# Pooled values in small tiles of their own, the gate written in place, and feature buffers moved by 32 bytes

## The chip, the cores and the metric

One NeuronCore of a Trainium2 chip runs the whole program. The metric is the device time of one execution in microseconds (us); a kernel's time is the median of several runs. Five engines work side by side, each with its own stream of instructions: TensorE (PE in the profile; its weight loads are PEld), VectorE (DVE), ScalarE (ACT), GpSimd (POOL) and SyncE (SP), which here only issues DMA transfers. They meet through semaphores.

## The reference

Attention with pooled keys and values over 8 batches of 8 heads (576 positions, 64 features each) is followed by two feed-forward layers over 4608 tokens of 512 features, everything in 32-bit floats.

```python
k_p = k.reshape(B, H, Sp, pool, D).mean(axis=3)      # pool = 8, Sp = 72
v_p = v.reshape(B, H, Sp, pool, D).mean(axis=3)
scores = scale * np.matmul(q, k_p.transpose(0, 1, 3, 2))
attn = softmax(scores)                               # over the 72 pooled positions
x = heads_to_features(np.matmul(attn, v_p))          # 4608 x 512

h = x @ w_in                                         # 512 -> 2048
x = (h * np.clip(h + 3.0, 0.0, 6.0) / 6.0) @ w_out   # 2048 -> 512

g = x @ w_gate                                       # 512 -> 1536
val = x @ w_val
return (g / (1.0 + np.exp(-g)) * val) @ w_out        # 1536 -> 512
```

## The kernel before

**Arithmetic.** Matmuls run in a reduced 32-bit type. Each operand is therefore cut into a high part (a rounding copy) and a low part (what is left), and a product takes three matmuls: high with high, high with low, low with high. `split` (L147, L148) makes the two parts: ACT copies the high one, VectorE subtracts for the low one. Three of the four large products also use a seven-product block scheme (Strassen's, with the names P1 to P7 for the products, 11 to 22 and S1 to S4 for the sums of features, 11 to 22 and T1 to T4 for those of weights).

**Stages.** (1) Start-up, to about 125 us: attention of the first 512 tokens. (2) To about 603 us: nine blocks of 512 tokens. For each block 16 iterations of the `up` product (`mm3` at L616, 12 matmuls of 512 columns), and between them the attention of the next block. ACT writes the clipped part of an iteration's result to a tile `t` (L627, in `act1`), VectorE multiplies it by the result into `g` (L632, in `gate1`), and SP stores `g` to device memory (L636, `store_g`). In the loop `gate1` of an iteration runs in the next one, and its `store_g` in the one after that. (3) To about 969 us, the down stage: `down_b` (L885), 9 blocks of tokens x 7 products, each product 48 matmuls of 256 columns. (4) To the end: the second layer, with an up product of 384 columns (`mm3x` at L706) and a down product of 256 columns on the same line.

**One pair of heads ("a head" below: 32 of them, 4 for each batch) in stages 1 and 2.** SP loads the keys (`load_k`, L313), the values (`load_v` and `fetch_v`, L326 and L327, two DMAs into a tile of 128 pooled positions x 8 x 64) and the tail of the values (`load_vtail`, L333, three DMAs of the 16 pooled positions that don't fit in 128, each copy 32 partitions further on). The work of a head is cut into steps: RK and K pool and transpose the keys; R0 (`prep_v`) pools the values on POOL by three adds, 8 to 4 to 2 to 1 (L440 in `pool_v`), and writes the pooled row times a mask (L447) into slots 4 and 5 of the same value tile; R1 pools the tail with the same `pool_v`; R (`split_v`, L453 and L454) writes the high parts on ACT; Q (`split_v_lo`, L460 and L462) the low parts on VectorE and, as its last act, plans the loads of the values and the tail of the head three places on (`next_v`). Value tiles have three buffers, tails have three (`vts_t`).

**One unit of queries.** S scores (matmuls, L496 is one form), X and A exponentials, M (`scale_e`, L544, POOL) the division by the sum, E and F the tail of the exponentials (`split_tail`, and `lo_tail` at L559, on POOL and VectorE in turn), T the transposes on TensorE (`transpose_a`; L570 transposes the tail), U and L the copies to high and low parts, V the product with the values (`attend`, from L594), W and Y the writes of the high (L605) and low (L609) part of `x`. P (`prep_q`, L478) prepares queries, whose loads (`fetch_q`, L381) it plans two segments ahead.

**What sets the order.** The order of instructions on every engine is written out by the program (`manual_schedule`). A table `when` gives every step of a unit a place in time; sorting these gives one list of steps, `steps`, about twenty to a unit. `before(...)` asserts that a step comes ahead of another. Loads are not issued at once: a step puts them on a list `later` with a due count, `done[0] + 4` or `+ 8`, and they are emitted on SP's queue that many steps further on. SP works through its queue in order, so an instruction that waits holds up all behind it: on that one queue are the loads of q, k and v, the stores of `g`, and the loads and stores of the weight preparation (`prep_slot`: loads by `fetch_into`, L121; splits at L273 and L276; stores to `sup` and `sw` at L280 and L285).

**Weights and features of the down stage.** The features come back by `load_g` (L844) into tiles `gq`, and `split` makes from them the tiles `gb`, four buffers of 4 KB a partition, four `gb` tiles to a product. The seven weight blocks `pw` lie in big buffers that are free by then: one in a tile of its own, `px`, on the right side of memory, the others in the buffers of the up stage's weights (`wu`, four) and of `x` (two). The matmul takes its weights from `pw` and its moving operand from `gb`. `evac_b` (L901 and after it) takes the results.

**Start addresses.** From the memory plan of the built program, in bytes within a partition, and their remainder modulo 64: `wu` starts at 17088 + 16384 k (0), `x` at 82624 and 99008 (0), `gb` at 115392 + 4096 k (0), `px` at 178144 (32), `gq` at a remainder of 32. In the second layer the ring that holds `wr` and `xc` starts at 32, and `gc` at 0. The pools on the left side follow one another upwards (`wu`, `x`, `gb`, then `t` and its like), those on the right side downwards, so `px` lies above `gq`.

Of the kernel before, what the change touches and what calls it, by code (L numbers as in the profile page):

```python
# [8 lines left out]
F32 = mybir.dt.float32  # L9
# [14 lines left out]
def kernel(  # L24
# [47 lines left out]
    x_p = left_b.enter_context(tc.tile_pool(name="x", bufs=2))  # L72
    gb_p = left_b.enter_context(tc.tile_pool(name="gb", bufs=4))
# [10 lines left out]
    half = const.tile([P, 1], F32, name="half")  # L84

# [217 lines left out]
    vts_t = [a_p.tile([96, POOL, D], F32, name=f"vts{i}") for i in range(3)]  # L303
# [25 lines left out]
    def load_vtail(b, p, eng):  # L329
        v1 = v[b, 2 * p + 1].rearrange("(s o) d -> s o d", o=POOL)  # L330
        vts = vts_t[(b * KT + p) % 3]
        for i in range(3):
            eng.dma_start(out=vts[32 * i:32 * i + TAIL], in_=v1[P - SP_:])  # L333
        vt_t[b, p] = vts
# [102 lines left out]
    def pool_v(t):  # L437
        n = POOL // 2
        while n:
            nc.gpsimd.tensor_tensor(out=t[:, 0:n], in0=t[:, 0:n], in1=t[:, n:2 * n], op=ALU.add)  # L440
            n //= 2

    def prep_v(b, p):
        t = v_t.pop((b, p))
        pool_v(t)
        m = t[:, 4:6]
# [178 lines left out]
    def act1(ps):  # L625
        t = t_p.tile([P, N], F32, tag="t", name="t")
        nc.scalar.activation(out=t, in_=ps, func=ACTF.Relu, bias=half, scale=1.0 / 6.0)  # L627
        return t

    def gate1(t, ps):  # L630
        g = t_p.tile([P, N], F32, tag="g32", name="g32", bufs=4)
        nc.vector.scalar_tensor_tensor(out=g, in0=t, scalar=1.0, in1=ps, op0=ALU.min, op1=ALU.mult)  # L632
        return g
# [388 lines left out]
    for i, h in ((i, head_no[u[0], p]) for i, u in enumerate(units) for p in u[1]):  # L1022
# [8 lines left out]
        if h + 3 < len(heads) and h >= KT - 1:  # L1031
            before(("Q", h), ("R1", h + 3))
    for i, u in enumerate(units):
# [34 lines left out]
    def next_v(i):  # L1068
        for load in (load_vtail, load_v):
            for h in next_heads(i, 3):  # L1070
                later.append((done[0] + 4, lambda load=load, h=h: load(*heads[h], nc.sync)))

    def do_step(st):
# [9 lines left out]
        elif what == "R0":  # L1083
            prep_v(*heads[i])
        elif what == "R1":
            pool_v(vt_t[heads[i]])
        elif what == "R":
            split_v(*heads[i])
        elif what == "Q":
            split_v_lo(*heads[i])  # L1090
            next_v(i)
        elif what == "P":
            prep_q(segs[i])
            for n in ((KT, KT + 1) if i == KT - 1 else (i + 2,)):
                if KT <= n < len(segs) and i >= KT - 1:
                    later.append((done[0] + 4, lambda n=n: load_q(segs[n], sync4)))
# [40 lines left out]
    with tc.manual_schedule():  # L1137
# [64 lines left out]
        for j in range(NB):  # L1202
            for f in range(F1):
                if (j, f) == (NB - 1, 0):
# [4 lines left out]
                    new_pw(0, lb["px"].tile([P, BIG], F32R, tag="px", name="pw"))  # L1209
# [125 lines left out]
```

## Time and profile before

| | |
|---|---|
| runs | 1761.25, 1763.97, 1765.88 us (median 1763.97) |
| the profiled execution | 1764.89 us |
| its span in the profile | 1763.1 us |
| mean granted clock of TensorE | 0.988 |
| busy share of the span | PE 97%, PEld 91%, DVE 76%, ACT 43%, POOL 36% |
| matmuls | 11116 |
| bytes moved | 432.47 MB, 245 GB/s on average |

Times in the profile are microseconds from the start of the span. Matmuls are pipelined, so the busy time that a row gives for one matmul (some 280 ns) is longer than the pitch at which they follow each other; where TensorE runs without a gap, the busy time of a group divided by its count is the pitch. The granted clock is a share of full speed (1.00 is 2.4 GHz). In rows of waits and groups, "<-DVE gb L142" names the engine, tile and line that ended the wait. An issue of a DMA on SP is written SPq.

### The profile page before, as it was taken

Reading aid. Unit: us, or ns where it says so; the run is one execution under the profiler, and the core shown is the slowest. Engines: PE = TensorE matmul, PEld = TensorE weight load, DVE = VectorE, ACT = ScalarE, POOL = GpSimd, SP = SyncE. Lnnn points to the kernel's source line nnn. Section 1 sums busy time; section 2 is a strip of 40 time slices with the busy share of each in tenths; the row PEclk is TensorE's granted clock in tenths of the full one; section 3 lists DMA queues with packets and bytes.
Section 4 is the critical chain, followed back from the end, with each engine's and each line's share of the span. In section 5 each row is a group of like instructions: output and inputs, shape, how many; then the busy total and the mean of one; then the engine's idle time right before and its main releaser. Section 6 shows DMA issues by size and latency. Waiting matters only on the chain.

```text
span 1763.1 us, 30766 instructions
## 1 busy us (share of the span) xinstructions
PE 1705.5 (97%) x11116; PEld 1608.8 (91%) x11116; DVE 1333.7 (76%) x2356; ACT 753.8 (43%) x1656; POOL 638.4 (36%) x822
## 2 busy tenths in 40 slices
PE   5889998999999999999999999999999999999999
PEld 3678887878788899999999999999999999999999
DVE  6797887888875678888888668668668668668666
ACT  5565554545544445555554224224224224224223
POOL 6565666666722000000000550550550550550560
PEclk9799999999999999999999999999999999999999
DMA  6776888878767974555565778878878878878876
GB/s 162 183 188 171 245 257 259 243 256 247 223 223 255 413 308 150 187 208 196 194 213 200 263 249 269 313 244 272 314 240 281 307 243 278 310 244 276 275 239 215
DMA packets 235832, 432.47 MB, mean 245 GB/s; under 512 B 86688, under 2 KB 168608, under 8 KB 218528
## 3 DMA queue, kind: packets, MB, share of 16 engines
q1 hardware_dynamic: 234624, 430.25, 73.9%
q8 instruction: 88, 1.44, 0.3%
q14 instruction: 64, 0.52, 0.1%
q10 hardware_dynamic: 1056, 0.26, 0.1%
HBM read 326.11 MB, written 104.33 MB: 244 GB/s over the span
## 4 chain that ended last, share of the span: by engine, by line
PE 76%; DMA 3%; DVE 3%; issue 1%; ACT 1%; SPq 0%; POOL 0%; DVEq 0%; ACTq 0%; POOLq 0%
PE b L706 45%; PE b L885 19%; PE h L616 10%; DMA g<-g 2%; PE pss L496 1%; DMA gq<-g 1%; DVE g L632 1%; PE pst L570 0%; DVE s L276 0%; PE pst L566 0%; DMA q_in<-in_q_dram 0%; SPq L381 0%; DVE q L139 0%; DVE xc L148 0%; PE psv L594 0%
## 5 line engine op out<-in xcount | busy, mean ns | idle before, releaser
L706 PE MATMUL b<-xc,wr 128*128 128x384 f32 x3024 | 526.3, 334 | 3.5 <-ACT xc L147 2.3
L706 PEld LDWEIGHTS b<-xc,wr 128*128 128x128 f32 x3024 | 523.9, 188 | 4.7 <-ACT xc L147 3.1
L616 PE MATMUL h<-x,wu 128*128 128x512 f32 x1728 | 435.3, 403 | 4.7 <-DVE g L632 2.6
L753 POOL TENSOR_TENSOR s<-s,c 128x384 f32<-128x384 f32 x144 | 142.4, 1014 | 756.6 <-ACT s L751 756.6
L715 DVE TENSOR_TENSOR c<-c,b 128x384 f32<-128x384 f32 x504 | 264.9, 552 | 174.7 <-PE b L706 151.0
L616 PEld LDWEIGHTS h<-x,wu 128*128 128x128 f32 x1728 | 322.7, 192 | 72.3 <-DVE g L632 4.9
L885 PEld LDWEIGHTS b<-gb,pw 128*128 128x128 f32 x3024 | 362.2, 191 | 0.5 <-DVE gb L148 0.4
L885 PE MATMUL b<-gb,pw 128*128 128x256 f32 x3024 | 362.5, 283 | 0.2 <-DVE gb L148 0.2
L706 PE MATMUL b<-wr,gc 128*128 128x256 f32 x2268 | 265.6, 279 | 0.0
L706 PEld LDWEIGHTS b<-wr,gc 128*128 128x128 f32 x2268 | 265.4, 188 | 0.0
L147 ACT CAST gb<-gq 128x512 fp32r<-128x512 f32 x252 | 156.1, 621 | 170.1 <-PE b L885 159.8
L148 DVE TENSOR_TENSOR gb<-gq,gb 128x512 fp32r<-128x512 f32 x252 | 168.1, 688 | 55.4 <-ACT gb L147 54.7
L760 POOL TENSOR_TENSOR gf<-s,c 128x384 f32<-128x384 f32 x144 | 168.2, 1191 | 66.4 <-DVE c L715 64.4
L147 ACT CAST gc<-gf 128x768 fp32r<-128x768 f32 x126 | 105.7, 839 | 187.1 <-POOL gf L760 100.9
L751 ACT ACTIVATE s<-c 128x384 f32<-128x384 f32 x144 | 73.5, 526 | 198.4 <-DVE c L715 197.3
L148 DVE TENSOR_TENSOR gc<-gf,gc 128x768 fp32r<-128x768 f32 x126 | 134.1, 1093 | 16.3 <-ACT gc L147 13.9
L627 ACT ACTIVATE t<-h,half 128x512 f32<-128x512 f32 x144 | 98.9, 687 | 79.9 <-PE h L616 60.7
L632 DVE SCALAR_TENSOR_TENSOR g<-t,h 128x512 f32<-128x512 f32 x144 | 97.4, 678 | 30.4 <-DMA g<-g 20.0
L723 ACT COPY c<-b 128x384 f32<-128x384 f32 x72 | 33.9, 471 | 127.5 <-PE b L706 127.5
L863 DVE TENSOR_TENSOR gq<-gq 128x1024 f32<-128x1024 f32 x72 | 87.7, 1219 | 0.0
L544 POOL TENSOR_TENSOR e<-e,sm 128x288 f32<-128x288 f32 (+4 forms) x74 | 48.0, 649 | 101.9 <-DVE sm L540 73.6
L205 DVE TENSOR_TENSOR gf<-gf 128x768 f32<-128x768 f32 (+1 forms) x66 | 66.9, 1029 | 12.1 <-POOL gf L760 10.9
(103 smaller groups left out, 1655.7 us busy)
## 6 DMA issues: line engine op xcount, KB each, us to landing
wr<-sup SPq DMA_DIRECT2D x72, 1024.0 KB
wr<-sdn SPq DMA_DIRECT2D x84, 768.0 KB
wr<-sup SPq DMA_DIRECT2D x72, 768.0 KB
g<-g SPq DMA_DIRECT2D x144, 256.0 KB
gq<-g SPq DMA_DIRECT2D x36, 1024.0 KB
sup<-s SPq DMA_DIRECT2D x12, 1792.0 KB
wstg<-in_moe_w_out_dram SPq DMA_DIRECT2D x56, 256.0 KB
sw<-s SPq DMA_DIRECT2D x8, 1792.0 KB
```

Of the source, the lines that this page charges most:

```text
L147: nc.scalar.copy(out=hi, in_=src)
L148: lo_engine.tensor_tensor(out=lo, in0=src, in1=f32(hi), op=ALU.subtract)
L616: nc.tensor.matmul(out=ps, lhsT=w(kt, wh), rhs=x(kt, xh), start=first and n == 0, stop=last and n == 3 * len(kts) - 1,)
L627: nc.scalar.activation(out=t, in_=ps, func=ACTF.Relu, bias=half, scale=1.0 / 6.0)
L632: nc.vector.scalar_tensor_tensor(out=g, in0=t, scalar=1.0, in1=ps, op0=ALU.min, op1=ALU.mult)
L706: nc.tensor.matmul(out=ps, lhsT=w(wh), rhs=x(xh), start=first and n == 0, stop=last and n == 2)
L715: add = lambda dst, a, b: nc.vector.tensor_tensor(out=dst, in0=a, in1=b, op=ALU.add)
L751: nc.scalar.activation(out=g[q], in_=c[q], func=ACTF.Sigmoid)
L753: nc.gpsimd.tensor_tensor(out=g[q], in0=g[q], in1=c[q], op=ALU.mult)
L760: nc.gpsimd.tensor_tensor(out=gf[p][:, GP[TURN[q]], f], in0=g[q], in1=c[q], op=ALU.mult)
L863: nc.vector.tensor_tensor(out=v(what), in0=v(a), in1=v(b), op=op)
L885: nc.tensor.matmul(out=ps[:, d], lhsT=w[:, CB * c + k, wh, P * d:P * (d + 1)], rhs=g[:, gh, k], start=what == place and (c, d, k, m) == (0 ...
```

## The change

The change has four parts.

- `pool_v` takes its output as an argument. The values are pooled into slot 0 of the value tile, and the product with the mask goes to a new small tile `vm` (three buffers) instead of slots 4 and 5. The pooled tail goes to a new small tile `vtp` (three buffers). So the value tile is last read by POOL in R0, and the tail's by POOL in R1.
- `next_v` is now planned by R0 for the values (three heads on) and by R1 for the tail (two heads on), each still due four steps later; the tails have two buffers instead of three. The loads of q are due after eight steps instead of four.
- `act1` writes to the tile with the tag `g32`, five buffers, and `gate1` multiplies in place; the two buffers of `t` go.
- A tile `gap` of 8 floats (32 bytes a partition) lies ahead of `gb`, and `px` is 8 floats longer, of which the first 4096 are used.

```diff
@@ -70,6 +70,7 @@
     left_b, l1, l1_ps = ExitStack(), ExitStack(), ExitStack()
     wu_p = left_b.enter_context(tc.tile_pool(name="wu", bufs=4))
     x_p = left_b.enter_context(tc.tile_pool(name="x", bufs=2))
+    gap_p = left_b.enter_context(tc.tile_pool(name="gap", bufs=1))
     gb_p = left_b.enter_context(tc.tile_pool(name="gb", bufs=4))
     t_p = l1.enter_context(tc.tile_pool(name="t", bufs=2))
     ps_y = l1_ps.enter_context(tc.tile_pool(name="ps_y", bufs=1, space=PSUM))
@@ -82,6 +83,7 @@
 
     ident = const.tile([P, P], F32, name="ident")
     half = const.tile([P, 1], F32, name="half")
+    gap_p.tile([P, 8], F32, name="gap")
 
     BIG = 4096
 
@@ -300,7 +302,7 @@
     kbd_t = [a_p.tile([P, K2], F32, name=f"kbd{p}") for p in range(KT)]
     vst_t = [a_p.tile([P, 2, P], F32R, name=f"vst{p}") for p in range(KT)]
     vtl_t = [a_p.tile([96, P], F32R, name=f"vtl{p}") for p in range(KT)]
-    vts_t = [a_p.tile([96, POOL, D], F32, name=f"vts{i}") for i in range(3)]
+    vts_t = [a_p.tile([96, POOL, D], F32, name=f"vts{i}") for i in range(2)]
     vmask = a_p.tile([P, 2, 1], F32, name="vmask")
     et_t = [a_p.tile([P, MAXQ, 96], F32, name=f"et{i}") for i in range(NE)]
     sm_t = [a_p.tile([P, 2 * MAXQ, 3], F32, name=f"sm{i}") for i in range(3)]
@@ -328,7 +330,7 @@
 
     def load_vtail(b, p, eng):
         v1 = v[b, 2 * p + 1].rearrange("(s o) d -> s o d", o=POOL)
-        vts = vts_t[(b * KT + p) % 3]
+        vts = vts_t[p % 2]
         for i in range(3):
             eng.dma_start(out=vts[32 * i:32 * i + TAIL], in_=v1[P - SP_:])
         vt_t[b, p] = vts
@@ -434,16 +436,20 @@
                 in_=ps[D * h2:D * h2 + D], func=ACTF.Copy, scale=c,
             )
 
-    def pool_v(t):
-        n = POOL // 2
-        while n:
-            nc.gpsimd.tensor_tensor(out=t[:, 0:n], in0=t[:, 0:n], in1=t[:, n:2 * n], op=ALU.add)
-            n //= 2
+    def pool_v(t, out):
+        for n in (4, 2, 1):
+            nc.gpsimd.tensor_tensor(
+                out=t[:, :n] if n > 1 else out, in0=t[:, :n], in1=t[:, n:2 * n], op=ALU.add)
+
+    def pool_tail(b, p):
+        t = a_p.tile([96, 1, D], F32, tag="vtp", name="vtp", bufs=3)
+        pool_v(vt_t[b, p], t)
+        vt_t[b, p] = t
 
     def prep_v(b, p):
         t = v_t.pop((b, p))
-        pool_v(t)
-        m = t[:, 4:6]
+        pool_v(t, t[:, :1])
+        m = a_p.tile([P, 2, D], F32, tag="vm", name="vm", bufs=3)
         nc.gpsimd.tensor_tensor(
             out=m, in0=t[:, 0:1].to_broadcast([P, 2, D]), in1=vmask.to_broadcast([P, 2, D]), op=ALU.mult
         )
@@ -623,14 +629,13 @@
         mm3(ps, lambda kt, a: w[:, a, kt], lambda kt, a: x[:, kt, a], range(KT), True, True)
 
     def act1(ps):
-        t = t_p.tile([P, N], F32, tag="t", name="t")
+        t = t_p.tile([P, N], F32, tag="g32", name="g32", bufs=5)
         nc.scalar.activation(out=t, in_=ps, func=ACTF.Relu, bias=half, scale=1.0 / 6.0)
         return t
 
     def gate1(t, ps):
-        g = t_p.tile([P, N], F32, tag="g32", name="g32", bufs=4)
-        nc.vector.scalar_tensor_tensor(out=g, in0=t, scalar=1.0, in1=ps, op0=ALU.min, op1=ALU.mult)
-        return g
+        nc.vector.scalar_tensor_tensor(out=t, in0=t, scalar=1.0, in1=ps, op0=ALU.min, op1=ALU.mult)
+        return t
 
     def store_g(j, f, g):
         nc.sync.dma_start(out=g_d[j][:, :, f // NP1, f % NP1], in_=g.rearrange("p (r n) -> p r n", r=2))
@@ -1028,8 +1033,9 @@
             before(("V", i), ("R", h + 4))
         if h + 2 < len(heads):
             before(("K", h), ("RK", h + 2))
-        if h + 3 < len(heads) and h >= KT - 1:
+        if h + 3 < len(heads):
             before(("Q", h), ("R1", h + 3))
+            before(("Q", h), ("R0", h + 3))
     for i, u in enumerate(units):
         if i + 1 < NU:
             for what in "SXAE":
@@ -1065,10 +1071,9 @@
         for h in next_heads(i):
             later.append((done[0] + 8, lambda h=h: load_k(*heads[h], nc.sync)))
 
-    def next_v(i):
-        for load in (load_vtail, load_v):
-            for h in next_heads(i, 3):
-                later.append((done[0] + 4, lambda load=load, h=h: load(*heads[h], nc.sync)))
+    def next_v(i, load, ahead):
+        for h in next_heads(i, ahead):
+            later.append((done[0] + 4, lambda h=h: load(*heads[h], nc.sync)))
 
     def do_step(st):
         what, i = st
@@ -1082,18 +1087,19 @@
                 next_k(i)
         elif what == "R0":
             prep_v(*heads[i])
+            next_v(i, load_v, 3)
         elif what == "R1":
-            pool_v(vt_t[heads[i]])
+            pool_tail(*heads[i])
+            next_v(i, load_vtail, 2)
         elif what == "R":
             split_v(*heads[i])
         elif what == "Q":
             split_v_lo(*heads[i])
-            next_v(i)
         elif what == "P":
             prep_q(segs[i])
             for n in ((KT, KT + 1) if i == KT - 1 else (i + 2,)):
                 if KT <= n < len(segs) and i >= KT - 1:
-                    later.append((done[0] + 4, lambda n=n: load_q(segs[n], sync4)))
+                    later.append((done[0] + 8, lambda n=n: load_q(segs[n], sync4)))
         elif what == "S":
             scores(units[i])
         elif what == "N":
@@ -1206,7 +1212,7 @@
                     for nm in ("px", "gq"):
                         lb[nm] = right_b.enter_context(
                             tc.tile_pool(name=nm, bufs=1, side="right", reuse_waits="tile"))
-                    new_pw(0, lb["px"].tile([P, BIG], F32R, tag="px", name="pw"))
+                    new_pw(0, lb["px"].tile([P, BIG + 8], F32R, tag="px", name="pw")[:, :BIG])
                     new_pw(1, big_x("pw"))
                 hp = ps_h.tile([P, N], F32, tag="h", name="h")
                 up(hp, wu[f], x_tile(j))
```

## Rows read from the trace of the kernel before

**Rows 1.** Windows by stage: length, busy PE, PEld, DVE, ACT, POOL, clock, DMA, GB/s
```profile
0.00:125.00 125.00, 89.50 (x432) 71.13 (x433) 97.21 (x220) 75.53 (x303) 71.81 (x129) 0.90 0.71 175
125.00:603.00 478.00, 463.60 (x2371) 386.88 (x2371) 369.14 (x833) 244.75 (x631) 256.05 (x405) 0.98 0.78 249
603.00:969.00 366.00, 363.52 (x3031) 362.95 (x3029) 307.63 (x434) 186.75 (x306) 0.00 (x0) 1.00 0.60 215
969.00:1763.00 794.00, 788.85 (x5286) 787.81 (x5286) 559.68 (x871) 246.77 (x417) 310.55 (x288) 1.00 0.79 268
```
**Rows 2.** Costliest groups: count, busy us, mean ns of one, idle before and releaser
```profile
L885 PE MATMUL b<-gb,pw 128*128 128x256 f32 x3024 | 362.5, 283 | 0.2 <-DVE gb L148 0.2
L706 PE MATMUL b<-wr,gc 128*128 128x256 f32 x2268 | 265.6, 279 | 0.0
```
**Rows 3.** Windows of L885 alone, two blocks: length, PE, PEld, clock, DMA, GB/s
```profile
643.29:648.96 5.67, 5.67 (x50) 5.67 (x49) 1.00 0.87 308
654.71:660.47 5.76, 5.76 (x50) 5.76 (x49) 1.00 0.02 4
```
**Rows 4.** Window of L706 alone within a down product, the same columns
```profile
1068.00:1088.00 20.00, 20.00 (x174) 20.00 (x173) 1.00 0.79 255
```
**Rows 5.** Timeline of PE at L570's waits: start, length, instruction, [idle before, releaser]
```profile
287.73 0.66 PE L570 MATMUL pst<-ident,et 128*96 128x128 f32 x2 [4.19 <-POOL et L559]
357.22 0.55 PE L570 MATMUL pst<-ident,et 96*96 96x96 f32 x2 [1.89 <-POOL et L559]
419.48 0.31 PE L570 MATMUL pst<-ident,et 128*96 128x128 f32 x1 [1.40 <-POOL et L559]
484.37 0.34 PE L570 MATMUL pst<-ident,et 64*96 64x64 f32 x1 [3.60 <-POOL et L559]
```
**Rows 6.** Timeline of POOL at the first and the fourth of them
```profile
278.38 1.67 POOL L440 TENSOR_TENSOR vts<-vts 96x256 f32<-96x256 f32 x3
284.38 2.60 POOL L440 TENSOR_TENSOR v_in<-v_in 128x256 f32<-128x256 f32 x3 [4.33 <-DVE x L609]
477.60 1.99 POOL L440 TENSOR_TENSOR vts<-vts 96x256 f32<-96x256 f32 x3
482.01 1.65 POOL L440 TENSOR_TENSOR v_in<-v_in 128x256 f32<-128x256 f32 x3 [2.42 <-DVE vtl L462]
```
**Rows 7.** Timeline of POOL and of SP's issues ahead of the first
```profile
257.14 0.40 POOL L447 TENSOR_TENSOR v_in<-v_in,vmask 128x128 f32<-128x128 f32 x1
281.30 0.39 SPq L326 DMA_DIRECT2D v_in<-in_v_dram  x1
```
**Rows 8.** Windows around the stalls, the columns of the first group
```profile
262.00:283.54 21.54, 21.10 (x109) 17.31 (x107) 20.91 (x46) 12.50 (x31) 15.00 (x25) 1.00 0.87 258
283.54:287.73 4.19, 0.01 (x1) 0.01 (x1) 3.20 (x5) 0.54 (x3) 3.11 (x6) 0.74 0.69 178
287.73:293.00 5.27, 5.27 (x15) 4.22 (x16) 2.04 (x6) 1.69 (x5) 2.70 (x5) 0.56 0.89 304
357.22:362.00 4.78, 4.78 (x17) 4.09 (x18) 3.75 (x9) 1.59 (x5) 2.70 (x5) 0.64 0.50 153
484.37:491.00 6.63, 6.63 (x21) 5.35 (x22) 2.94 (x8) 2.03 (x6) 5.29 (x9) 0.55 0.96 306
```
**Rows 9.** Timeline of POOL and of SP's issues around 464 us
```profile
466.41 0.40 POOL L447 TENSOR_TENSOR v_in<-v_in,vmask 128x128 f32<-128x128 f32 x1
463.06 1.19 SPq L636 DMA_DIRECT2D g<-g  x2
```
**Rows 10.** SP's waits, 0 to 60 us: total us, count, longest
```profile
SPq L121 <- DVE gb L142: 6.7, 2, 4.2
```
**Rows 11.** Waits of DVE and SP, 125 to 603 us; a DMA group
```profile
DVE g L632 <- DMA g<-g: 17.8, 8, 4.9
SPq L381 <- DVE mx L506: 37.8, 15, 4.8
sup<-s SPq DMA_DIRECT2D x12, 1792.0 KB
```

## The prediction

> **What bounds the kernel now.** I read the stretches first [rows 1]. TensorE is busy 363.5 of 366.0 us in the down stage and 788.9 of 794.0 us after it: there only a faster matmul helps. Start-up keeps it busy 89.5 of 125.0 us, and the attention stretch (125 to 603 us) 463.6 of 478.0 us at a granted clock of 0.98. So time can come from two places: the pitch of the matmuls, and 14.4 us of idle with what the low clock costs behind it.
>
> The pitch. Two groups have one form, 128 x 128 weights against 256 columns [rows 2]: L706 needs 265.6 us / 2268 = 117.1 ns, L885 362.5 / 3024 = 119.9 ns, and neither waits (idle 0.0 and 0.2 us). Inside L885 the blocks of 48 matmuls differ too [rows 3]: the first block of an iteration, the one with the `px` weights, takes 5.67 us (118.1 ns each), the next ones 5.76 us (120.0). In the memory plan these are the only L885 matmuls whose two operands start 32 bytes apart modulo 64; the L706 group with 256 columns is also 32 apart, and a pure stretch of it [rows 4] holds 174 matmuls in 20.00 us, of which some 2.5 only overlap an edge: 116.6 ns.
>
> The idle. Of TensorE's waits in the attention stretch 11.1 us are four waits of the tail transposes (L570) for POOL's L559: 4.19, 1.89, 1.40 and 3.60 us [rows 5], each at the fourth head of a batch. POOL isn't slow there, it waits: at 280.05 us it has finished the tail's pooling and stands 4.33 us until L440 can start on the value tile [rows 6]. The view names DVE as releaser, but the load explains it: its issue on SP starts at 281.30 us [rows 7], though the tile's previous values were pooled by 257.54 us. The load waited for step Q of the head three places earlier (and four steps more), while batches 4 to 7 put their heads one unit apart. The other three stalls repeat this.
>
> **The change part by part.**
>
> Down stage. `gb` moves from 0 to 32 modulo 64, the `px` weights from 32 to 0; the other weights stay at 0. Then all 63 blocks have weights at 0 and moving operand at 32, which is exactly the pairing of the 117 ns group. At 116.7 ns a block takes 48 x 116.7 = 5.60 us: 54 x (5.76 - 5.60) = 8.6 us, and 9 x (5.67 - 5.60) = 0.6 us, together 9.3 us. The other end is the `px` block itself, which is 32 apart the other way round: 54 x 0.09 = 4.9 us. I take 9.3, as the L706 row has the same remainders on both operands. The cover holds: DVE, which makes the low halves, is busy 307.6 of 366 us [rows 1], 84%, which rises to 86%; were it late, the gain would go into waits at L885.
>
> The measured blocks show that the start address matters. A rule of the Trainium skill speaks against it: "SBUF — State Buffer", section "Who interferes with whom", gives TensorE two independent read ports, one for the moving operand and one for weights, and says that it never waits on anyone; by that the shift brings 0 and the sum below is 9.3 us smaller. No clause there knows of a remainder modulo 64, while the two rows [rows 3] differ; the measurement decides.
>
> Value loads. POOL's instructions stay the same in kind, shape and number; only where the last add and the masking product write changes. The value tile is then read for the last time by the product (L447) and not by L460, so the load for head h+3 goes out after R0(h) + 4 steps instead of Q(h) + 4. For the first stall that is about 263 us (I placed it among SP's instructions by program order) instead of 281.30 us, some 17 us ahead of the need at 280.05. The tails lose a buffer (three to two), yet their load moves to R1(h) + 4 for head h+2: step 690 in place of 695 for the head of the first stall, so equally early; and POOL has not waited for tails in these four places. POOL then takes the 2.6 + 0.4 us of value work and L559 before TensorE asks at 283.54 us: 4.2 us saved. By the same reckoning 1.9 and 1.4 us. At the fourth, POOL finishes its tail only at 479.59 us [rows 6]; 1.65 + 0.40 us of value work and L559 end by about 481.9 us, while TensorE is ready at 480.77 us: about 1.2 us stays, 2.4 are saved. Sum 9.9 us.
>
> The clock behind them. After three of the stalls the granted clock falls [rows 8]: 0.56 over 5.27 us, 0.64 over 4.78, 0.55 over 6.63, so part of each runs at 1.2 instead of 2.4 GHz right after TensorE stood still. At full clock the same work takes 2.3 + 1.7 + 3.0 = 7.0 us less. After the stall of 1.40 us I see no such fall, so the 1.2 us that stays should cost none.
>
> What the moved loads pass. Per head 2 DMAs of some 0.39 us of SP time [rows 7] and 3 for the tail go out earlier, ahead of q loads, weight loads and gate stores; their number doesn't change. New is that SP waits for POOL's pooling. Laying program order over the trace, SP gets there before POOL at some five of 25 heads, the worst at 463.7 us against 466.81 [rows 9]: 3.1 us in which the next q loads, weight loads and stores stand behind it. Before, the same queue waited for DVE at L381 alone 37.8 us [rows 11], which the four steps more for the q loads shorten. I take 0 with bounds of -3 and +3 us. At start-up twelve value DMAs (5 us of issue) move to about 30 to 38 us, where SP waits 6.7 us in all for a staging buffer [rows 10]: 0, bounds -2 and +0.3.
>
> Gate in place. No instruction is added; a tile of 2 KB goes. The wait for the store of five tiles ago, issued three iterations before, moves from DVE's L632 (17.8 us in 8 waits, the longest 4.9 [rows 11], six of them after 560 us, when TensorE is full anyway) to ACT's L627, half an iteration later. Behind L627 on ACT stand exponentials, the copies of transposed weights and the rescaling of weights; DVE's evacuations are freed of it. I take 0, bounds -0.5 (TensorE's own short waits for L632) and, as a rival, the cost below.
>
> Sum: 9.3 + 9.9 + 7.0 = 26.2 us. The profiled execution took 1764.9 us (span 1763.1), so 1738.7; the median of the runs is 0.9 lower, which gives 1738 us.
>
> **The rivals.**
>
> VectorE becomes the bound in the bursts. From 262 to 283.54 us it is busy 20.91 of 21.54 us [rows 8], 97%. From 262 to 293 us it does 20.9 + 3.2 + 2.0 = 26.1 us of work; at 97% that needs 26.9 us, so the first burst could give back only 31 - 26.9 = 4.1 of its 6.5 us, 63%. On all four: 10.6 instead of 16.9, 1745 us. Against it: DVE was on pace when TensorE stopped, its x evacuation (L609) starting as soon as ACT's copy was done.
>
> The address does nothing, and the difference between the blocks comes from something else in them: 16.9 us alone, 1747 us. It would need another reason for [rows 3], which I don't have.
>
> Slower: ACT blocks on stores. Each of the 20 prepared-weight stores up to 603 us (1792 KB; 12 of them in [rows 11], 8 under another name) delays the 256 KB gate store queued behind it. If ACT waited the mean of today's DVE waits (2.2 us) at each, with TensorE standing for all of it, that is 44 us, so 1738 + 44 = 1782 us. It decides once a store costs TensorE over 26.2 / 20 = 1.3 us. Against it: a delayed gate is needed by the up step three iterations on, one later than today, and ACT is half idle (244.8 of 478 us [rows 1]).
>
> **How the numbers follow.** Forecast 0.60 (own range 1733 to 1745: down stage 4.9 to 9.3, queue and start-up bounds), VectorE 0.24, address 0.08, slower 0.06, the rest 0.02. The range 1730 to 1752 takes in the first three with the bounds. A difference of 0.3%, 5.3 us, is about what a measurement of this kernel can tell from none. Faster 0.90: the three faster cases, less 0.02 for VectorE eating everything while the address gives half. Same 0.05, slower 0.05.
>
> **What would show it.** The down stage: every block of 48 at 5.60 us, the L885 group at 353 us in place of 362.5; 5.67 us means the weaker end, 5.76 the address rival. The stalls: POOL's L440 without idle before the value tiles, no L570 wait above 1.5 us, attention stretch at 461 us in place of 478. If L570 or L594 wait for DVE instead, VectorE took over; if L627 shows idle for stores of g and TensorE waits right behind, the slow rival. A new long SP wait for L447 with q loads late behind it would make the prediction wrong in a way that I price at 3 us only.

## The result and the profile after

The changed kernel takes 1749.47 us (median of 4 runs, 1746.81 to 1752.37), the kernel before beside it 1764.74: a ratio of 0.9917, with a 95% interval from 0.9894 to 0.994. It is 15.3 us faster, where 26 were forecast. The profiled execution of after took 1746.81 us (span 1745.0), that of before 1764.89 (span 1763.1); this pair of traces lies 18.1 us apart.

The windows by stage, with borders at the same instructions in both traces (first `up` matmul of the second block, first and last L885 matmul, which is L890 in the changed kernel, and the 295th matmul of the second layer); columns as in [rows 1]. The kernel before:

```profile
0.00:131.80 131.80, 96.30 (x467) 76.92 (x468) 102.64 (x232) 78.13 (x310) 78.12 (x140) 0.91 0.72 177
131.80:602.90 471.10, 456.70 (x2334) 381.03 (x2334) 363.71 (x820) 242.14 (x624) 249.75 (x395) 0.98 0.78 249
602.90:965.40 362.50, 362.33 (x3025) 362.05 (x3025) 304.93 (x430) 185.88 (x304) 0.00 (x0) 1.00 0.60 215
965.40:1021.00 55.60, 52.07 (x296) 50.90 (x296) 37.88 (x63) 15.62 (x28) 26.14 (x25) 1.00 0.75 256
```

The changed kernel:

```profile
0.00:128.30 128.30, 96.64 (x467) 77.49 (x468) 102.37 (x232) 78.13 (x310) 77.27 (x139) 0.87 0.73 184
128.30:589.20 460.90, 449.94 (x2334) 376.74 (x2333) 364.70 (x820) 242.41 (x624) 251.02 (x395) 1.00 0.81 253
589.20:942.60 353.40, 353.12 (x3025) 352.90 (x3023) 304.77 (x431) 185.05 (x304) 0.00 (x0) 1.00 0.60 215
942.60:1003.00 60.40, 55.15 (x297) 53.58 (x296) 38.37 (x63) 15.90 (x28) 26.18 (x25) 0.94 0.80 277
```

From stage to stage: start-up -3.5 us, attention -10.2, down stage -9.1, and the turn to the second layer **+4.8**. What follows takes 742.1 and 742.0 us. Together that is the 18.1 us between these two traces; the medians, 15.3 us apart, are the measure. TensorE is idle for 11.0 us of the attention stretch (460.9 - 449.9), where it was idle for 14.4; its busy time there falls by 6.8 us for the same matmuls, which is the clock (0.98 before, 1.00 after).

The down group, which answers to [rows 2], and two of its blocks, as in [rows 3]:

```profile
L890 PE MATMUL b<-gb,pw 128*128 128x256 f32 x3024 | 353.3, 279 | 0.3 <-DVE gb L150 0.3
```

```profile
628.50:634.10 5.60, 5.60 (x50) 5.60 (x49) 1.00 1.01 394
634.10:639.70 5.60, 5.60 (x50) 5.60 (x49) 1.00 0.55 202
```

TensorE's waits from 125 to 610 us (total, count, longest), in the changed kernel and then in the kernel before:

```profile
PE h L622 <- DVE g L637: 5.6, 6, 1.8
PE psv L600 <- DVE x L615: 3.2, 4, 1.1
PE pst L576 <- POOL et L565: 2.0, 2, 1.6
```

```profile
PE pst L570 <- POOL et L559: 11.1, 4, 4.2
PE psv L594 <- DVE x L609: 1.7, 2, 0.8
PE h L616 <- DVE g L632: 1.3, 3, 0.5
```

The waits for POOL went from 11.1 to 2.0 us, but those for VectorE rose from 3.0 to 8.8. At the turn TensorE now waits for weights (timelines of the changed kernel: PE, then SP's issues of `wr`, and SP's wait ahead of them):

```profile
944.94 6.38 PE L711 MATMUL b<-xc,wr 128*128 128x384 f32 x25 [2.13 <-DMA wr<-sup]
...
954.98 0.44 PE L711 MATMUL b<-xc,wr 128*128 128x384 f32 x1 [2.17 <-ACT xc L149]
```

```profile
938.68 2.15 SPq L690 DMA_DIRECT2D wr<-sup  x4
```

```profile
SPq L690 <- DVE gb L150: 13.7, 1, 13.7
```

The down stage ends at 942.8 us, so the first `wr` load goes out 4 us ahead of that. In the kernel before it went out 10 us ahead, at 955.53 against 965.6, and TensorE did not wait for it:

```profile
955.53 6.13 SPq L685 DMA_DIRECT2D wr<-sup  x4
```

### The profile page after: what moved, and what is told of

Same layout as the page of the kernel before. It is cut to its first block, busy times and chain, and to the rows that moved or that the text cites. A ratio compares the mean times of both kernels' runs of the same rounds, so it can differ in the third digit from the quotient of the medians.

```text
span 1745.0 us, 30719 instructions
## 1 busy us (share of the span) xinstructions
PE 1692.8 (97%) x11116; PEld 1598.5 (92%) x11116; DVE 1334.7 (76%) x2356; ACT 753.4 (43%) x1656; POOL 639.0 (37%) x821
## 4 chain that ended last, share of the span: by engine, by line
PE 79%; DVE 8%; DMA 7%; POOL 2%; ACT 2%; issue 1%; SPq 1%; DVEq 0%; POOLq 0%; ACTq 0%
PE b L711 45%; PE b L890 19%; PE h L622 12%; DMA q_in<-in_q_dram 1%; DVE g L637 1%; PE pss L502 1%; DMA qv<-in_q_dram 1%; DMA wstg<-in_moe_w_out_dram 1%; DMA gq<-g 1%; DMA y<-o 1%; DVE mx L512 1%; POOL v_in L441 1%; DMA k_in<-in_k_dram 1%; DVE s L278 1%; DVE qT L484 1%
## 5 line engine op out<-in xcount | busy, mean ns | idle before, releaser
L622 PE MATMUL h<-x,wu 128*128 128x512 f32 x1728 | 428.7, 400 | 6.8 <-DVE g L637 6.8
L890 PEld LDWEIGHTS b<-gb,pw 128*128 128x128 f32 x3024 | 353.1, 188 | 0.6 <-DVE gb L150 0.5
L890 PE MATMUL b<-gb,pw 128*128 128x256 f32 x3024 | 353.3, 279 | 0.3 <-DVE gb L150 0.3
L633 ACT ACTIVATE g<-h,half 128x512 f32<-128x512 f32 x144 | 99.0, 687 | 69.7 <-PE h L622 57.5
L637 DVE SCALAR_TENSOR_TENSOR g<-g,h 128x512 f32<-128x512 f32 x144 | 97.4, 677 | 20.2 <-ACT g L633 19.2
L550 POOL TENSOR_TENSOR e<-e,sm 128x288 f32<-128x288 f32 (+4 forms) x74 | 48.1, 650 | 117.7 <-DVE sm L546 95.6
```

Source lines behind the costliest of these rows:

```text
L622: nc.tensor.matmul(out=ps, lhsT=w(kt, wh), rhs=x(kt, xh), start=first and n == 0, stop=last and n == 3 * len(kts) - 1,)
L637: nc.vector.scalar_tensor_tensor(out=t, in0=t, scalar=1.0, in1=ps, op0=ALU.min, op1=ALU.mult)
L890: nc.tensor.matmul(out=ps[:, d], lhsT=w[:, CB * c + k, wh, P * d:P * (d + 1)], rhs=g[:, gh, k], start=what == place and (c, d, k, m) == (0 ...
```

## The experiments

**The turn.** The memory plan of the changed kernel suggests a cause. Longer by 8 floats, `px` pushes the `gq` tiles below it down by 32 bytes. The ring that later holds `wr` did not move. Before, its two lower tiles (161760 and 169952) lay on two `gq` tiles to the byte; now the first of them, which ends at 169952, overlaps by 32 bytes the `gq` tile that starts at 169920, and that one is read by the very last split of the down stage. Two runs take the shift apart. The first has the shift alone, on the kernel before:

```diff
+    gap_p = left_b.enter_context(tc.tile_pool(name="gap", bufs=1))
+    gap_p.tile([P, 8], F32, name="gap")
...
-new_pw(0, lb["px"].tile([P, BIG], F32R, tag="px", name="pw"))
+new_pw(0, lb["px"].tile([P, BIG + 8], F32R, tag="px", name="pw")[:, :BIG])
```

> Only the 32-byte shift (gap ahead of gb, px longer by 8 floats) on the kernel before. Theory: two effects of opposite sign. Every block of 48 down matmuls takes 5.60 us, the L885 group 353.3 us in place of 362.5 (-9.2 us). And the turn from the down stage to the second layer loses 4.7 us, because the gq tiles moved by 32 bytes too: the first tile of the weight ring now overlaps the gq tile that is split last, so the first wr load is issued about 4 us before the end of the down stage instead of 10. Net -4.5 us: 1760 us where the kernel before takes 1764.5. Rival: the turn lost time for another reason (the VectorE chain of the first x sums, reached earlier, or the values part); then the first wr load goes out about 10 us before the end of the down stage and the net is -9.2 us: 1755 us. The attention stretch is as before, with four waits of TensorE for L559.

Measured: 1761.76 us, ratio 0.9985 (0.9975 to 0.9996). Its stages from the attention stretch on, and SP's first issues of `wr`:

```profile
132.40:604.00 471.60, 457.06 (x2334) 380.94 (x2333) 365.12 (x820) 241.92 (x624) 250.72 (x395) 0.98 0.78 250
604.00:959.60 355.60, 355.26 (x3024) 354.70 (x3024) 304.51 (x430) 185.75 (x304) 0.00 (x0) 1.00 0.59 211
959.60:1019.70 60.10, 54.59 (x297) 52.69 (x296) 38.29 (x63) 15.95 (x28) 26.13 (x25) 0.97 0.79 278
```

```profile
955.72 1.99 SPq L687 DMA_DIRECT2D wr<-sup  x4
```

The turn takes 60.1 us, the first load goes out 4 us ahead of the end: the shift does it. The down stage gave 6.9 us in this trace and not 9.1; what was different in it is told in the last section.

The second leaves the shift out of the changed kernel (the same lines the other way round).

> The changed kernel without the shift: no gap tile, px without the 8 floats more. Theory: down matmuls take 362.5 us again (+9.2), the first wr load is issued 10 us before the end of the down stage and the 4.7 us of the turn come back, so 1749.5 + 4.5 = 1754 us: about 10.5 us faster than the kernel before, all of it up to 603 us (3.5 in start-up, 10 in the attention stretch). Rival (the turn is not the shift's doing): 1749.5 + 9.2 = 1758.7 us.

Measured: 1752.23 us, ratio 0.9941 (0.9929 to 0.9952). The stages: attention 461.0 us, down stage 361.8, turn 55.8. So the rest of the change is worth 11.3 us by the medians, and the shift, which should bring 9, only some 2 to 3 more.

The third takes back the length of `px` alone; `gb` stays moved.

```diff
-new_pw(0, lb["px"].tile([P, BIG + 8], F32R, tag="px", name="pw")[:, :BIG])
+new_pw(0, lb["px"].tile([P, BIG], F32R, tag="px", name="pw"))
```

> The changed kernel with px at its old length and place (remainder 32), while gb stays moved. The gq tiles are back at their old addresses and match the ring's tiles to the byte. Theory: the first wr load goes out about 10 us before the end of the down stage, TensorE's 2.1 us wait for wr and the low clock behind it go, -4.7 us; the 9 blocks with px weights have both operands at 32 and take 5.76 us instead of 5.60, +1.4 us; net 1749.5 - 3.3 = 1746 us. Rival (the turn is set by VectorE's chain of sums, which the faster down stage only reaches sooner): 1749.5 + 1.4 = 1751 us. A third reading, that the px remainder itself does not matter for matmuls with gb at 32, would leave those 9 blocks at 5.60 us.

Measured: 1749.72 us, ratio 0.9922 (0.991 to 0.9934). In the trace the turn is back (56.2 us, and the first load goes out at 937.83 us, 9.5 ahead of the end at 947.3), and the block with `px` takes 5.70 us beside 5.60 (windows of L890 alone, with edges rounded to 0.1 us, then the turn). Over the nine such blocks the matmuls follow each other every 119.7 to 120.0 ns, 5.75 us to a block.

```profile
592.60:598.30 5.70, 5.70 (x48) 5.70 (x48) 1.00 1.03 429
598.30:603.90 5.60, 5.60 (x50) 5.60 (x49) 1.00 1.01 397
```

```profile
947.30:1003.50 56.20, 53.16 (x298) 52.58 (x297) 38.22 (x63) 15.72 (x28) 26.16 (x25) 0.97 0.74 257
```

Both parts came as expected (-4.2 and +1.3 us), but the time did not fall by 3; the attention stretch of this trace took 464.1 us, 3.2 more than in the first trace of after, with 6.8 us at the low clock, which that one had not. The medians of these two kernels don't show the turn, the traces do.

**The attention stretch.** One thing stands out in VectorE's timeline (changed kernel): 4.3 us of waiting for queries ahead of the first burst, and 4.05 us ahead of the second.

```profile
273.96 0.18 DVE L546 RECIPROCAL sm<-sm 128x4 f32<-128x4 f32 x1
278.47 0.51 DVE L484 STREAM_TRANSPOSE qT<-q_in 128x320 f32<-128x320 f32 x1 [4.32 <-DMA q_in<-in_q_dram]
```

On SP these loads stand behind 1 MB of weights for the preparation:

```profile
265.61 5.41 SPq L123 DMA_DIRECT2D wstg<-in_moe_w_out_dram  x4
271.12 2.69 SPq L383 DMA_DIRECT2D q_in<-in_q_dram  x4
```

Due after four steps they would stand ahead of them, as before. Two theories follow: the late queries make VectorE late, or VectorE has too much to do in the bursts whatever the queries do.

```diff
-                    later.append((done[0] + 8, lambda n=n: load_q(segs[n], sync4)))
+                    later.append((done[0] + 4, lambda n=n: load_q(segs[n], sync4)))
```

> The changed kernel with the q loads due after four steps again instead of eight. Theory A (the later q loads fall behind a weight step's 1 MB of loads on SP's queue, VectorE stands 4.3 and 4.1 us for them at L484 ahead of two bursts, and TensorE then waits for the late VectorE): VectorE's two waits for q_in go, TensorE's waits right behind them (1.1 + 1.8 us near 285, 1.0 + 1.2 + 1.2 us near 350 to 363) go too, idle in the attention stretch falls from 10.6 to about 4.5 us, 1749.5 - 6 = 1743.5 us. Theory B (VectorE has simply too much work in the bursts, whatever the q loads do): the sum of TensorE's waits for L637 and L615 stays within 1.5 us of 11.8, and the time within 1.5 us of 1749.5. Down stage and second layer the same under both.

Measured: 1747.22 us, ratio 0.9914 (0.9901 to 0.9927). VectorE's waits for queries are gone, and TensorE is as idle as with them, 10.6 us of the stretch (its window, then TensorE's waits in it):

```profile
128.70:589.00 460.30, 449.74 (x2334) 376.46 (x2334) 367.48 (x819) 242.92 (x624) 249.86 (x395) 1.00 0.80 254
```

```profile
PE h L622 <- DVE g L637: 4.2, 4, 1.4
PE psv L600 <- DVE x L615: 3.8, 4, 1.7
PE pst L576 <- POOL et L565: 2.4, 2, 1.6
```

The waits moved to other places and kept their sum, 8.0 us for VectorE (8.8 by the same view in the trace of after, not the 11.8 that the expectation names). The late queries were visible, and not the cause of TensorE's waits. The time fell by 2 to 3 us all the same, between the 6 us of the one theory and the 1.5 us of the other. The traces don't show where, and with the memory plan mended, below, the same step gave 1.2 us: whether it is worth anything stays open.

The second theory starts from how busy VectorE is where TensorE waits for it. Around the longest of these waits (1.82 us, up to 288.27 us) the changed kernel shows it busy for 6.75 of 7.00 us; columns as in [rows 1]:

```profile
283.00:290.00 7.00, 5.17 (x27) 4.17 (x27) 6.75 (x16) 2.40 (x8) 0.92 (x2) 1.00 0.60 160
```

It was tested by taking work off VectorE (the low parts of the prepared weights are left out):

```diff
-            nc.vector.tensor_tensor(out=t[:, part, 1], in0=q[:, part], in1=f32(t[:, part, 0]), op=ALU.subtract)
+            if u < PREP_A:
+                nc.scalar.copy(out=t[:, part, 1], in_=q[:, part])
+            else:
+                nc.vector.tensor_tensor(out=t[:, part, 1], in0=q[:, part], in1=f32(t[:, part, 0]), op=ALU.subtract)
```

> The changed kernel with 43 us of work taken off VectorE in the attention stretch: the low part of the prepared weights (L278, two operations of 1.22 and 0.95 us for each of 20 units) is left out, ACT writes a copy in its place (the low parts hold the wrong values, all transfers stay). If VectorE's work bounds the bursts, TensorE's waits for L637 and L615 (8.9 us) fall to under 4, the attention stretch shortens by 5 us or more from 460.9, and the time by as much, to 1744 us. If the bursts are bound by the late q loads or by ACT, the waits stay at 8 to 10 us or move to ACT, and the time stays within 2 us of 1749.5.

Measured: 1745.14 us, ratio 0.9882 (0.9867 to 0.9898). The window of the stretch and TensorE's waits in it:

```profile
133.60:587.90 454.30, 449.80 (x2335) 376.18 (x2335) 321.48 (x781) 273.13 (x664) 237.04 (x395) 1.00 0.81 257
```

```profile
PE h L625 <- DVE g L640: 3.2, 5, 1.5
PE psv L603 <- DVE x L618: 1.2, 2, 0.7
```

VectorE works 43 us less (321.5 against 364.7), the stretch is 6.6 us shorter, TensorE's idle time falls to 4.5 us and its waits for VectorE to 4.4, a little above the 4 that were expected; the view lists none for POOL any more. In the other kernels with the values part the idle time lies between 8.7 and 11.2 us, whatever else was changed. Two rivals are still there in this trace: VectorE waits 7.9 us for queries, and POOL 5.6 us for tails of values, and TensorE's idle time fell in spite of them. VectorE's work in the bursts is what holds the stretch now, for some 6.5 us.

**The gate in place**, alone on the kernel before:

```diff
     def act1(ps):
-        t = t_p.tile([P, N], F32, tag="t", name="t")
+        t = t_p.tile([P, N], F32, tag="g32", name="g32", bufs=5)
...
     def gate1(t, ps):
-        g = t_p.tile([P, N], F32, tag="g32", name="g32", bufs=4)
-        nc.vector.scalar_tensor_tensor(out=g, in0=t, scalar=1.0, in1=ps, op0=ALU.min, op1=ALU.mult)
-        return g
+        nc.vector.scalar_tensor_tensor(out=t, in0=t, scalar=1.0, in1=ps, op0=ALU.min, op1=ALU.mult)
+        return t
```

> Only the gate in place on the kernel before: relu into the g32 tile, five buffers, multiplied in place. Theory: VectorE's 17.8 us of waits for stores at L632 go, ACT waits some 9 us for stores at L627 instead, TensorE sees neither: the attention stretch stays at 471 us with its four waits for L559, the time within 1.5 us of the kernel before. Rival of the prediction (ACT blocks on stores): the stretch gets longer by more than 2 us, with TensorE waiting behind L627. Third reading: freeing VectorE of its waits is itself worth something in the bursts: the stretch gets shorter by 2 us or more.

Measured: 1763.02 us beside 1765.07, ratio 0.999 (0.9982 to 0.9999): 2.05 us faster, a little more than the 1.5 us expected. The stretch takes 469.9 us (471.1 in the kernel before), with the four waits for L559 (10.8 us). ACT waits 5.7 us for stores at L627, VectorE no longer does, TensorE notices neither. The values part could not be tried alone: with the two `t` tiles kept, the left pools would reach 144064 bytes, above `kbd0`, which lies at 143936 once the small tiles are there. The gate's 2 KB are the room for them.

**The changed kernel once more**, to see what of its trace repeats.

> The changed kernel once more, beside the runs of this group: 1749.5 us (1746.8 to 1752.4 so far). What it is to show: which parts of its profile repeat. The down stage must again have a pitch of 116.9 ns and the turn a late first wr load. If the start-up again ends near 128.3 us, the 3.5 us against the kernel before are the change's; if near 132, they are chance of the clock. The same for the low clock in the attention stretch (none in the first profile).

Measured: 1750.4 us, ratio 0.9916 (0.99 to 0.9933).

```profile
0.00:133.60 133.60, 101.99 (x467) 82.11 (x468) 103.24 (x232) 78.50 (x310) 77.42 (x139) 0.86 0.70 177
133.60:595.40 461.80, 451.30 (x2335) 377.65 (x2334) 366.56 (x820) 242.47 (x624) 251.17 (x395) 1.00 0.80 253
```

Start-up takes 133.6 us in this trace, 128.3 in the first, so the 3.5 us of the first pair can't be put down to the change. In the ten traces of kernels with the values part it ends at 128.3 to 130.0 us seven times and at 131.9 to 133.6 three times, in the three without it at 131.8 to 132.4: whether a part of it is the change's stays open. The attention stretch (461.8), the down pitch (116.9 ns) and the turn (59.9) repeat.

**Versions meant to be faster.** The first mends the memory plan by length: `px`, `gq` and the ring's tiles get 64 bytes more per 8 KB, so that they coincide again, with the start remainders modulo 64 of the changed kernel, and q loads after four steps.

```diff
-        return l2["ring"].tile([P, 2048], F32R, tag="wr", name="wr")
+        return l2["ring"].tile([P, 2048 + 16], F32R, tag="wr", name="wr")
...
-new_pw(0, lb["px"].tile([P, BIG + 8], F32R, tag="px", name="pw")[:, :BIG])
+new_pw(0, lb["px"].tile([P, BIG + 32], F32R, tag="px", name="pw")[:, 8:8 + BIG])
```

> q loads due after four steps, and the memory plan mended: px, the gq tiles and the ring's tiles are each 64 bytes longer per 8 KB, so that a ring tile again covers one gq tile (or half of px) to the byte, while all start remainders of the down stage stay as in the changed kernel. Theory: down blocks at 5.60 us, and the turn at 56 us in place of 60 as in the runs without the overlap: 4 us less than the run with the q loads alone (1747.2), 1743 us. If the turn depends on something else in px than the overlap, it stays at 60 us and the time at 1747.

Measured: 1755.9 us, ratio 0.9948 (0.9935 to 0.9961): slower than the changed kernel. The turn is mended (56.6 us), but every matmul group that reads one of the longer tiles got slower. The costliest groups of this run, then the same lines of the changed kernel:

```profile
L711 PE MATMUL b<-xc,wr 128*128 128x384 f32 x3024 | 531.8, 337 | 3.0 <-ACT xc L149 2.5 <-DVE xc L150 0.5
L890 PE MATMUL b<-gb,pw 128*128 128x256 f32 x3024 | 354.7, 280 | 0.0
L711 PE MATMUL b<-wr,gc 128*128 128x256 f32 x2268 | 269.5, 281 | 0.0
```

```profile
L711 PE MATMUL b<-xc,wr 128*128 128x384 f32 x3024 | 529.1, 336 | 5.2 <-ACT xc L149 2.2
L711 PE MATMUL b<-wr,gc 128*128 128x256 f32 x2268 | 265.6, 279 | 0.0
```

So a remainder modulo 64 doesn't describe the effect: the remainders are the same, the times are not. The next run rests on that rule all the same: it puts weights and moving operand 32 apart modulo 64 in the two groups where they were equal (two of its lines; the `x` buffers, where two of the seven `pw` blocks lie, move with it, and so does `gb`).

```diff
-            t = ring_tile()
+            t = ring_tile()[:, 8:]
...
-        return x_p.tile([P, BIG], F32R, tag="x", name=name)
+        return x_p.tile([P, BIG + 16], F32R, tag="x", name=name)
```

> The same, and the remainders of the other two equal pairs set as in the down stage: x tiles start at 32 modulo 64 against up weights at 0 (1728 matmuls of 512 columns), and in the second layer the up weights start at 0 against xc at 32 (3024 of 384 columns). If the start address costs a matmul 3.3 ns whenever both operands have the same remainder, whatever the columns: the 384-column group takes 3024 x 3.3 = 10 us less (about 519 us in place of 529), the up group has a pitch of 223.3 ns in place of 226.7 (5.8 us less, of which the attention stretch may keep some as waits for VectorE): 1743 - 13 = 1730 us. If the effect belongs to 256 columns alone: 1743 us.

Measured: 1759.44 us, ratio 0.9975 (0.9963 to 0.9986). The 384-column group takes 532.1 us and not 519, and the `up` group (512 columns) 435.0 us beside 430.2 in the run before, the down group 356.7 beside 354.7: the expectation was wrong, and with the wrong sign for 512 columns.

The last two runs mend the plan by order: `gq` lies above `px`, its tiles fall on the ring's tiles in the order in which they come free, and no distance between weights and moving operand changes.

```diff
-                    for nm in ("px", "gq"):
+                    for nm in ("gq", "px"):
...
+                    for slot in range(4):
+                        gq["first", slot] = new_gq(slot)
```

> The changed kernel with the gq tiles placed above px, so that each of the ring's four tiles covers one gq tile to the byte, in the order in which they come free; px keeps remainder 0, and every distance between weights and moving operand is that of the changed kernel (32 modulo 256 in both 256-column groups, 0 in the two others). Theory: first wr load about 15 us before the end of the down stage, the turn at 56 us instead of 60, down stage 353.3 us, second layer 738.0 us: 1750 - 4.3 = 1745.5 us. If the turn depends on more than the overlap, it stays at 60.

> The same with the q loads due after four steps. With q loads after four steps alone the time was 1747.2 us against 1749.5 to 1750.4 of the changed kernel, and TensorE's idle time in the attention stretch was the same (10.5 us): so 1743 to 1745.5 us; equal to the run before within 1 us if that difference was chance.

Measured: 1745.92 us, ratio 0.9897 (0.9876 to 0.9919), and with q loads after four steps 1744.75 us, ratio 0.9884 (0.9872 to 0.9897). From the trace of the first, SP's issues and TensorE at the turn:

```profile
930.66 11.52 SPq L690 DMA_DIRECT2D wr<-sup  x4
```

```profile
945.84 1.21 PE L711 MATMUL b<-xc,wr 128*128 128x384 f32 x6
```

The first load goes out 15 us ahead of the down stage's end at 945.8 us, TensorE takes up the second layer without a wait for it, and the turn takes 56.3 us. The last version is 20.3 us faster than the kernel before it ran beside, some 5 more than the change as it was made.

## Why the prediction was right and where it failed

The measured time lies within the range, near its upper end, and the change is faster as forecast. By its steps:

- **Down stage, 9.3 us forecast: right.** The group fell by 9.2 us, both kinds of blocks take 5.60 us, and the rival "the address does nothing" is out. In the run with `px` back at its old place both operands of its block start at 32, and that block alone stays slow. The weaker end, weights at 32 and moving operand at 0, was not run apart. VectorE's cover held: 0.3 us of waits. What saved the step is that its price was taken from a row of the same form, 256 columns with the same operands' places; the rule read from it ("32 apart modulo 64") was wrong as a rule: the runs with longer tiles have blocks 96, 160 and 224 apart, which are 32 apart modulo 64 too, at 117.5 to 120.0 ns. That the shift made the very pairing of the L706 row is why the sum came out.
- **The four waits, 9.9 us forecast: right at their place, wrong in what comes next.** They fell by 9.1 us, from 11.1 to 2.0. But the stretch's idle time fell by 3.4 us only (by 3.2 to 5.7 in the other traces of kernels with the values part and VectorE's full work), since VectorE was late next. So the step that failed is the sum "9.9 us", which counts each wait as gained in full and leaves VectorE's bound to the rival. The condition of that rival was in [rows 8], 20.91 of 21.54 us busy; the forecast set it aside because VectorE kept pace up to the first stall. The run with less work on VectorE shows that it was the right reading. Its price fits better than its parts do: 10.6 us for waits and clock together, where these two traces give 10.2 and 9.3 and all traces of kernels with the values part, VectorE's full work and the `up` operands where they were 7.0 to 10.8. (By its own sum it comes to 1744 us, not 1745.) It cut both by the same share, to 63%; in the first trace the clock came back almost whole (6.8 of 7.0 us) and of the waits a third (3.4 of 9.9).
- **The clock, 7.0 us forecast: right.** The same matmuls of the stretch were busy for 6.8 us less at 1.00 than at 0.98. In the second trace (461.8 us) it was 5.4: there the clock fell once more, behind waits of 1.6 and 1.8 us that end at 289.8 and 295.6 us (0.66 over 295 to 300 us). Over all traces of kernels with the values part TensorE is at the low clock for 0 to 6.8 us of the stretch, in the three without for 13.7 to 17.1.
- **What the moved loads pass, 0 within 3 us: right for SP, incomplete for the queries and the tails.** SP waited for POOL's product 2.9 us in all. Its wait for free query tiles at L381 (L383 in the changed kernel) fell from 37.8 [rows 11] to 8.1 us, as said. That the later queries come behind a weight load, and VectorE then stands for 8.4 us, was not costed; the traces show no wait of TensorE that goes with it, and the 1 to 3 us between the medians stay open. The tails were to come equally early; POOL now waits 5.2 us for them in two waits, the longer one (4.1 us) up to 279.52 us, in the first burst. The run with less work on VectorE has such waits too (5.6 us), with TensorE idle for 4.5 us only.
- **The gate, 0: right** to some 2 us (2.05 us faster by itself, 0.2 to 3.2 by the interval), and the slow rival (ACT blocks on stores) is out: 5.7 us of waits on ACT, none behind them.
- **Start-up, 0: not contradicted**; the traces of one and the same kernel end it at 128.3 and 133.6 us, so these runs can't price it closer.
- **The turn, not in the prediction: 4.3 to 4.8 us lost.** The 32 bytes were weighed for the matmuls, and not for what the moved tiles overlap later. Every tile behind `px` moves with it, and a later tile that covers one more of them by 32 bytes waits for its last reader.

So 26.2 became 15.3: 6.7 us (16.9 - 10.2; 7.6 in the second trace, part of it clock) went to VectorE's bound in the bursts and 4.3 to 4.8 to the turn. That the time lies within the range is in part luck: the range reached that far for the sake of the rivals and the weaker address, and the turn was not in it.

## What to carry to other kernels

When a stall is removed from a burst, look at the next engine's busy share inside the burst, not over the stage: at 97% it took two thirds of the waiting time that was freed here, and less work there gave it back. When a tile is moved by a few bytes, list what is placed on that memory later; a new overlap of 32 bytes is a whole new wait. A price for an address, like the 117 ns, holds for the form it was measured on; before it is used on another number of columns it has to be measured there.

## What the runs showed of the hardware

- **A matmul's pitch depends on the distance between moving operand and weights, in a way that changes with the number of columns.** From the traces of eight kernels (before, after, and six of the runs above), for matmuls that follow each other without idle time; the distance is that of the start addresses (moving minus weights) modulo 256, worked out from the memory plans:

| columns | columns / 2.4 GHz | mean pitch by distance |
|---|---|---|
| 256 | 106.7 ns | 0: 119.9 to 120.0; 32: 116.7 to 117.8; 96: 119.8 to 120.0; 160: 117.5 to 118.2; 224: 117.9 to 118.3 |
| 384 | 160.0 ns | 0, 64, 160, 224: 173.3 to 173.5; 32, 96: 176.5 to 176.7; 128: 176.1; 192: 176.6 |
| 512 | 213.3 ns | 0: 229.0 (most at 226 to 227); 32: 233.2; 96: 233.6 |

  The distance 32 is the best of those seen for 256 columns and among the worst for 384 and 512. For 256 columns the distance holds over several places of either operand. For 384 columns only the place of the weights varied modulo 256, and for 512 only that of the moving operand, so there the distance can't be told from that one address. Other distances were not tried, and why it is so stays open. The Trainium skill ("SBUF — State Buffer", section "Who interferes with whom") has TensorE's two reads independent; these rows differ from that.
- **At one and the same distance the pitch has more than one level, and each can last.** In the run with the shift alone the blocks have 116.6 ns up to a wait of 0.3 us for VectorE at 767.5 us, and 117.7 ns from there to the end of the stage; that is most of the missing part of its down stage. The wait by itself is not shown to be the cause: a wait of 0.3 us stands at the same block in the traces of the changed kernel and of five of its variants, and there the pitch is 116.6 to 116.7 ns on both sides of it. In the first run with longer tiles the first blocks at distance 32 have 117.7 ns, and from the second iteration on 116.7, without any wait. What sets the level stays open.
- **VectorE's integer work is slower beside POOL.** L141, the same 128 x 512 shift, in the changed kernel from 366 to 412 us, where POOL is busy 36 of 46 us, and from 480 to 589 us, where it is busy 21 of 109, and never beside one of the ten:

```profile
L141 DVE TENSOR_SCALAR q<-wstg 128x512 int32<-128x512 int32 x4 | 4.5, 1118 | 0.1
```

```profile
L141 DVE TENSOR_SCALAR q<-wstg 128x512 int32<-128x512 int32 x10 | 4.2, 423 | 0.3
```

  In this trace L141 takes 384 to 429 ns wherever no POOL instruction runs beside it, and up to 1416 ns where one does. POOL's side shows in the run with 43 us less work on VectorE: in the attention stretch the same 395 POOL instructions are busy for 237.0 us there, and for 251.0 in the changed kernel. So the two lengthen each other where they meet. The Trainium skill ("SBUF — State Buffer", section "Who interferes with whom") says that a tensor_scalar in a mode that uses both ports shares one pair with GpSimd and that the later of the two waits; the row agrees in direction, and no run here shows the mode of L141 or separates the two orders.
